# A ramp with x in transfers of 96 rows, its loads in another order, and roundings of the steps in two pieces

## The chip, the cores and the metric

The kernel runs on one core of one Trainium2 chip. The metric is the device time of one execution in microseconds, from the profiler; a kernel's time is the median of its runs.

## The reference, cut to what matters

A global filter in the frequency domain is followed by a two-layer perceptron with SiLU:

```python
X = np.fft.rfft(x, axis=1)                         # x: (8, 3008, 256), fp32
y = np.fft.irfft(X * (filt_r + 1j * filt_i)[None], n=3008, axis=1)
h = y.reshape(24064, 256) @ w_in                   # (256, 2048)
out = (h / (1 + exp(-h))) @ w_out                  # (2048, 256)
```

The weights `w_in` and `w_out` are float64 in memory; the kernel reads them as pairs of 32-bit words and rounds them to fp32 itself.

## The kernel before, in words

**Spectral part.** For each of the eight batches the transform of length 3008 = 2 x 47 x 32 is done in matrix products with tables. Stage 1 (`stage1`, line 308) multiplies x by a table `wx_t`; the results are copied out and written to a DRAM buffer d1 by the POOL queue (line 338). `load_t2` (line 404) reads them back in another order in six groups g; `forward` multiplies by the table `d_t` into banks `pb`, `multiply` (M) forms the products with the filters on VectorE (L433), `add` sums them (on GpSimd for batch 0, L441 and L442), `inverse` multiplies by `e_t` into banks `pc`, `even` copies (ScalarE, L465) and `rows` (VectorE, L473) forms sums and differences and sends them to a DRAM buffer d2. `load_t4` reads d2 and `stage3` (matrices `pd`) gives the tokens y.

**Perceptron.** The tokens of all batches are cut into 48 pairs of blocks; a pair takes eight steps, each with 128 x 2 columns of the hidden layer. Both products are done by Strassen's scheme with seven matrix products instead of eight: `hidden` (L611) and `project` (L670), whose instructions alternate in eight rounds per step. The pieces of the spectral part of the next batch are put into given steps and rounds by `put` and run by `until`.

**The ramp.** Batch 0 has nothing to hide behind: its spectral part, and the loading and rounding of the weights of the first nine column blocks j, are written out by hand ahead of the steps. The order of instructions on each engine is the order of the program text (a manual schedule). SyncE issues nearly all loads, so a load stands behind all loads written ahead of it; a transfer's issue also waits for the completion semaphore it takes over, of which there are eight, handed on in turn. `rounded(j)` calls `round_weights` (line 755): five operations on VectorE (L762, L764, L767, L768, L770), two on ScalarE (L763, L766), then two products that place the weights (L776, on GpSimd for j < 7, on VectorE from then on), and for odd j four combinations (`combine_weights`, L582). The blocks j = 9 to 15 are rounded inside steps 0 to 6, in round 1 of each.

**Batch 1.** Its x is loaded by `load_x` in eight pieces u, with the rows in two transfers of 64 and 32 rows; the first two are issued right ahead of step 0, the others by `stage1` itself, which stands in steps 0 to 7, round 3. `tokens` of pair 1 stands in step 6, round 1.

Of the kernel before, what the change touches and what calls it, by code (L numbers as in the profile page):

```python
# [55 lines left out]
NS, NG = 24, 6  # L56
# [35 lines left out]
def dft_tables():  # L92

    wf = np.zeros((128, 2, 64))
    for par in range(2):
        for i, idx in enumerate(ORDER):
            ph = 2 * np.pi * (np.arange(N1) * (2 * idx + par) % 94) / 94
            for h in range(2):
                wf[64 * h:64 * h + N1, par, 2 * i] = np.cos(ph)
                wf[64 * h:64 * h + N1, par, 2 * i + 1] = -np.sin(ph)  # L100

    wx = np.zeros((96, 2, 64))
    row = (np.arange(96) + 64) % 96
    for par in range(2):
        for i, idx in enumerate(ORDER):
            ph = 2 * np.pi * (row * (2 * idx + par) % 94) / 94
            wx[:, par, 2 * i] = np.where(row < 2 * N1, np.cos(ph), 0.0)
            wx[:, par, 2 * i + 1] = np.where(row < 2 * N1, -np.sin(ph), 0.0)  # L110

    wq = np.zeros((128, 4, 32))
    m = np.arange(24)
    for par in range(2):
        for i, idx in enumerate(ORDER):
            ph = 2 * np.pi * (m * (2 * idx + par) % 94) / 94
            for q in range(4):
                wq[32 * q:32 * q + 24, 2 * par, i] = np.where(m == 0, 0.5, np.cos(ph))  # L120
                wq[32 * q:32 * q + 24, 2 * par + 1, i] = -np.sin(ph)


    d = np.zeros((2, 2, 32, NS, 2, 32))
    n = np.arange(32)[:, None]
    for par in range(2):
        for i, idx in enumerate(ORDER):
            sp = 2 * idx + par
            kap = kept(sp)
            sg = np.where((kap - sp) % 94 == 0, 1.0, -1.0)  # L130
            k = np.where((kap - sp) % 94 == 0, kap, S - kap)
            th = 2 * np.pi * (n * k % S) / S
            d[par, 0, :, i, 0], d[par, 1, :, i, 0] = np.cos(th), np.sin(th)
            d[par, 0, :, i, 1], d[par, 1, :, i, 1] = -np.sin(th) * sg, np.cos(th) * sg


    e = np.zeros((4, 32, NG, 2, 2, 2, 32))
    n = np.arange(32)[None, :]
    for g in range(NG):
        for bank in range(2):  # L140
            for j in range(4):
                s = slot_residue(g, bank, j - j % 2)
                kap = kept(slot_residue(g, bank, j))
                sg = np.where((kap - s) % N1 == 0, 1.0, -1.0)[:, None]
                k = np.where((kap - s) % N1 == 0, kap, S - kap)[:, None]
                assert ((k - s) % 94 == (0 if j % 2 == 0 else N1)).all()
                th = 2 * np.pi * (n * k % S) / S
                e[j, :, g, bank, 0, 0], e[j, :, g, bank, 0, 1] = np.cos(th), np.sin(th)
                e[j, :, g, bank, 1, 0], e[j, :, g, bank, 1, 1] = -np.sin(th) * sg, np.cos(th) * sg


    wi = np.zeros((128, N1))
    for h in range(2):
        for i in range(NS):
            s = slot_residue(i // 4, i % 2, i // 2 % 2 * 2)
            ph = 2 * np.pi * ((2 * np.arange(N1) + h) * s % 94) / 94

            wi[64 * h + 2 * i] = 2 * np.cos(ph) / S if s else 1.0 / S
            wi[64 * h + 2 * i + 1] = -2 * np.sin(ph) / S if s else 0.0
    f32 = np.float32  # L160
    return (wf.astype(f32), wx.reshape(96, 128).astype(f32), wq.astype(f32), wi.astype(f32),
            d.reshape(128, NS, 2, 32).astype(f32),
            e.reshape(128, NG, 2, 2, 64).astype(f32))
# [3 lines left out]
def kernel(  # L167
# [51 lines left out]
    w_t = cpool.tile([128, 7, 2, NJP, 128], FP32)  # L219
    zero_t = w_t[:, S4, 0, NJP - 2:NJP].rearrange("p j n -> p (j n)")  # L220
    warm = cpool.tile([128, 1], FP32)
    bias_t = cpool.tile([128, 1], FP32)
    x_all = xpool.tile([128, 2, 2, 2 * C], FP32)
    x_t = [x_all[:, i] for i in range(2)]

# [37 lines left out]
    def spectral(b):  # L263
# [4 lines left out]

        def load_rows(view, u, n):


            for p0, r0, nr in ((32, 0, 64), (0, 64, 32)):
                nc.sync.dma_start(out=view[p0:p0 + nr],
                                  in_=bass.AP(tensor=x.tensor,
                                              offset=x.offset + (b * S + 32 * r0 + 4 * u) * C,
                                              ap=[[32 * C, nr], [1, 4 * n * C]]))

        def load_first():

            view = w_t.rearrange("p c w j n -> p (c w j n)")[:, 0:32 * C]  # L280
            for u, n in ((0, 2), (2, 2), (4, 4)):
                load_rows(view[:, 4 * C * u:4 * C * (u + n)], u, n)
            for u in range(8):
                xs[u] = view[:, 4 * C * u:4 * C * (u + 1)]
# [204 lines left out]
        def stage3(g):  # L489
# [3 lines left out]
            for cb in range(2):  # L493
                for i in range(4):
                    for c0 in (0, 64):
                        for h in range(2):
# [2 lines left out]
                                out=ps[h][c0:c0 + 64, cb, i, :],  # L499
                                lhsT=t4s[g][rows, i, 128 * cb + c0:128 * cb + c0 + 64],  # L500
                                rhs=wi_t[rows, :], start=True, stop=True)
            if g < 6 and (b > 0 or g > 1):
                load_t4(g + 2)
            if n0 == 0:
                y[b, half] = ypool.tile([128, 2, HALF], FP32, name=f"y_{b}_{half}", tag="y")
# [14 lines left out]
    def plan(b, part):  # L520
# [1 line left out]
        at = STEPS * b  # L522

        if b == 1:
            put(at - 51, 0, part["load_x"], 0)
            put(at - 51, 0, part["load_x"], 1)
            for u in range(8):
                put(at + u - 48, 3, part["stage1"], u)
        else:
# [225 lines left out]
    def round_weights(j):  # L755

        words = raws.pop(j).rearrange("p w (n t) -> p (w n) t", t=2)
        lo, hi = words[:, :, 0], words[:, :, 1]
        e = zpool.tile([128, 512], U32, name=f"e_{j}", tag="z")
        m = ppool.tile([128, 512], U32, name=f"m_{j}", tag="p")  # L760
        ef, mf = e.bitcast(FP32), m.bitcast(FP32)
        v.tensor_scalar(out=m, in0=hi, scalar1=0xfffff, scalar2=None, op0=ALU.bitwise_and)  # L762
        nc.scalar.activation(out=mf, in_=m, func=AFT.Identity, scale=2.0 ** -20, bias=1.0)  # L763
        v.tensor_scalar(out=e, in0=hi, scalar1=20, scalar2=0x7ff,  # L764
                        op0=ALU.logical_shift_right, op1=ALU.bitwise_and)
        nc.scalar.activation(out=ef, in_=e, func=AFT.Relu, bias=bias_t)  # L766
        v.scalar_tensor_tensor(out=mf, in0=lo, scalar=2.0 ** -52, in1=mf, op0=ALU.mult, op1=ALU.add)  # L767
        v.tensor_scalar(out=e, in0=ef, scalar1=255.0, scalar2=float(1 << 23),  # L768
                        op0=ALU.min, op1=ALU.mult)
        v.scalar_tensor_tensor(out=e, in0=hi, scalar=0x80000000, in1=e,  # L770
                               op0=ALU.bitwise_and, op1=ALU.bitwise_or)
        for w in range(2):
            cols = slice(256 * w, 256 * w + 256)
            dst = places(j, w) if w == 0 else places(j, w).rearrange("p k (q i) -> p k q i", q=4)
            eng = gp if j < 7 else v
            eng.tensor_tensor(out=dst, in0=columns(mf[:, cols], w), in1=columns(ef[:, cols], w),  # L776
                              op=ALU.mult)
        if j % 2:
            combine_weights(j // 2)
# [21 lines left out]
            if wide:  # L801
                load_weights(j)

    def rounded(j):
        if wide:
            round_weights(j)
        else:
            load_exact(j)

    def idle(n):  # L810
# [4 lines left out]

    def inverse_rows(part, g):
        part["inverse"](g)
        for i in range(2):
            part["even"](g, i)
            part["rows"](g, i)  # L820


    nc.sync.dma_start(out=wx_t, in_=wx_dram.ap())
    nc.vector.memset(zero_t, 0.0)
    nc.gpsimd.memset(bias_t, -896.0)
    nc.gpsimd.memset(x_all[96:128], 0.0)
    part = spectral(0)
    part["load_first"]()
    idle(6)
    nc.sync.dma_start(out=d_t[:, 0:8], in_=d_dram[:, 0:8])  # L830
    weights(0, 1)
    load_filters((nc.sync, nc.sync), 0, 4)
    weights(2, 3)
    for u in range(8):
        part["stage1"](u)
    for g in range(2):
        part["load_t2"](g)
    nc.sync.dma_start(out=d_t[:, 8:NS], in_=d_dram[:, 8:NS])
    nc.sync.dma_start(out=e_t, in_=e_dram.ap())
    for g in range(2, 4):  # L840
        part["load_t2"](g)
    for j in range(3):
        rounded(j)
    idle(16)
    for g in range(NG):
# [4 lines left out]
            part["add"](g, k)  # L850
        if g == 0:
            load_filters((nc.sync, nc.gpsimd), 4, 2 * NG)
            weights(4, 5)
        if g == 1:
            for t, dram in ((wi_t, wi_dram), (wf_t, wf_dram), (wq_t, wq_dram)):
                nc.sync.dma_start(out=t, in_=dram.ap())
        if g == 2:
            weights(6, 7, 8)
        if g > 0:
            inverse_rows(part, g - 1)  # L860
        idle(2)
# [3 lines left out]
    idle(12)  # L865
    for g in range(4):
        part["load_t4"](g)
    rounded(7)
    rounded(8)
    for g in range(4):  # L870
# [1 line left out]
    weights(9, 10, 11, 12, 13)  # L872
    early[0] = None
    plan_rest(0, part)
    for b in range(1, B):
        plan(b, spectral(b))
    for j in range(9, NJ):
        put(j - 9, 1, rounded, j)

        if j < 11:  # L880
            put(j - 9, 1, weights, j + 5)
# [5 lines left out]
    stores = (((10, 1), (10, 5)), ((19, 1), (23, 5)), ((31, 1), (31, 5)), ((35, 1), (35, 5)),  # L887
              ((43, 1), (43, 5)), ((50, 1), (51, 1)))
    for pair in range(len(pairs)):
        step, rnd = combines[pair % per]  # L890
        pending.append((pair // per * STEPS + step + rnd / ROUNDS, 98, lambda pair=pair: tokens(pair)))
        for chunk in range(2):
            step, rnd = stores[pair % per][chunk]
# [51 lines left out]
```

## Time and profile before

| | us |
|---|---|
| median of four runs | 2641.29 (2639.24 to 2644.06) |
| profiled execution | 2639.24 |
| its span | 2637.4 |
| PE busy | 2585.6 (98%) |
| DVE busy | 1700.7 (64%) |
| ACT busy | 1102.5 (42%) |
| POOL busy | 450.3 (17%) |
| mean granted clock | 0.986 |

The page divides the span into 40 slices of 66 us; the first two hold the ramp. A timeline row gives the start, the duration, the engine, the line, the operation with its tiles (`out<-in`), the number of instructions and, in brackets, the idle time of the engine before it with what released it. PE counts a matrix product of fp32 twice, as two passes. `SPq` and `ACTq` are the queues in which SyncE and ScalarE issue transfers.

### The profile page before, as it was taken

To read this page: it belongs to the slowest core of one execution; us is meant where nothing else is said; L and a number is where in the kernel's file an instruction comes from. 1 tells how busy PE (TensorE), PEld (TensorE's weight loads), DVE (VectorE), ACT (ScalarE), POOL (GpSimd) and SP (SyncE) were. 2 spreads that over 40 slices of the span, in tenths; PEclk is the share of its full clock that TensorE was granted. 3 is DMA by queue.
4 is the path that set the end of the run, shared out by engine and by line. 5 is a ranking of instruction groups with operands and counts; after the bars stand their busy time and mean duration, and the time that the engine had idled before them with its cause. 6 is when DMAs were issued, how large, how long until landed. Compare 5 with 4: busy or idle time off the path is not lost.

```text
span 2637.4 us, 48074 instructions
## 1 busy us (share of the span) xinstructions
PE 2585.6 (98%) x18748; PEld 2187.8 (83%) x18748; DVE 1700.7 (64%) x3585; ACT 1102.5 (42%) x3008; POOL 450.3 (17%) x692
## 2 busy tenths in 40 slices
PE   6799999999999999999999999999999999999998
PEld 3478888888888888888888888888888888888987
DVE  4666666667666666666666676666766666555554
ACT  1254344444444444444444444444444444444443
POOL 5211112211221111112111211121112111100100
PEclk8699999999999999999999999999999999999999
DMA  9632222322233123221222222232223311211000
GB/s 266 181 96 53 66 61 66 80 55 65 66 71 75 45 64 81 67 65 53 80 61 56 73 70 65 51 81 68 65 56 72 84 45 28 55 22 21 9 16 16
DMA packets 203659, 176.29 MB, mean 67 GB/s; under 512 B 122308, under 2 KB 176932, under 8 KB 202740
## 3 DMA queue, kind: packets, MB, share of 16 engines
q1 hardware_dynamic: 183144, 121.57, 19.3%
q0 software_dynamic: 17616, 48.52, 5.7%
q8 instruction: 147, 2.41, 0.4%
q10 hardware_dynamic: 2672, 3.13, 0.4%
q14 instruction: 80, 0.66, 0.1%
HBM read 98.15 MB, written 84.41 MB: 69 GB/s over the span
## 4 chain that ended last, share of the span: by engine, by line
PE 94%; DMA 3%; DVE 2%; SPq 1%; issue 0%; ACT 0%; POOL 0%; ACTq 0%; DVEq 0%
PE acc L670 43%; PE px L611 25%; PE pyz L611 19%; PE pd L498 3%; PE pb L421 2%; PE pc L454 2%; PE pf L388 1%; DMA raw<-in_moe_w_out_dram 1%; PE pa L330 0%; DMA x_all<-in_x_dram 0%; PE pa L321 0%; DMA d<-q 0%; DMA e_t<-e_tbl 0%; DMA w_t<-in_x_dram 0%; SPq L233 0%
## 5 line engine op out<-in xcount | busy, mean ns | idle before, releaser
L670 PE MATMUL acc<-g,w_t 128*128 128x256 f32 (+1 forms) x5376 | 1512.0, 375 | 0.4 <-DVE g L582 0.4
L670 PEld LDWEIGHTS acc<-g,w_t 128*128 128x128 f32 x5376 | 1021.3, 190 | 115.6 <-DVE g L582 0.8
L582 DVE TENSOR_TENSOR g<-pyz,abc 128x256 f32<-128x256 f32 (+1 forms) x1152 | 480.3, 417 | 551.7 <-ACT abc L632 304.5
L582 DVE TENSOR_TENSOR g<-g 128x256 f32<-128x256 f32 (+3 forms) x1152 | 617.0, 536 | 197.3 <-ACT g L615 184.1
L611 PE MATMUL px<-ty,w_t 128*128 128x256 f32 (+1 forms) x2304 | 686.9, 380 | 1.5 <-ACT abc L626 1.0
L615 ACT ACTIVATE g<-g 128x256 f32<-128x256 f32 (+1 forms) x1152 | 474.8, 412 | 246.1 <-DVE g L582 246.1
L582 POOL TENSOR_TENSOR s<-s 128x256 f32<-128x256 f32 (+1 forms) x329 | 259.8, 807 | 1453.5 <-DVE s L688 1373.0
L611 PEld LDWEIGHTS px<-ty,w_t 128*128 128x128 f32 x2304 | 424.1, 190 | 85.3 <-issue 25.9
L611 PE MATMUL pyz<-y,w_t 128*128 128x256 f32 (+1 forms) x1536 | 453.6, 377 | 2.9 <-DVE g L582 2.9
L611 PEld LDWEIGHTS pyz<-y,w_t 128*128 128x128 f32 x1536 | 283.7, 189 | 48.4 <-DVE g L582 7.9
L626 ACT COPY abc<-px 128x256 f32<-128x256 f32 (+1 forms) x384 | 141.8, 369 | 363.8 <-PE px L611 363.8
L615 ACT ACTIVATE g<-px 128x256 f32<-128x256 f32 (+1 forms) x384 | 146.5, 382 | 307.4 <-PE px L611 307.3
L632 ACT COPY abc<-px 128x256 f32<-128x256 f32 (+1 forms) x384 | 144.3, 376 | 309.2 <-PE px L611 309.2
L611 PE MATMUL px<-y,w_t 128*128 128x256 f32 (+1 forms) x768 | 229.8, 381 | 1.0 <-ACT y L246 1.0
L611 PE MATMUL pyz<-ty,w_t 128*128 128x256 f32 (+1 forms) x768 | 225.6, 375 | 0.0
L611 PEld LDWEIGHTS px<-y,w_t 128*128 128x128 f32 x768 | 142.1, 189 | 40.0 <-ACT g L615 15.5
L611 PEld LDWEIGHTS pyz<-ty,w_t 128*128 128x128 f32 x768 | 146.0, 190 | 16.9 <-DVE g L582 0.5
L619 ACT COPY abc<-px 128x256 f32<-128x256 f32 (+1 forms) x384 | 135.7, 353 | 2.7 <-PE px L611 1.3
L244 DVE COPY y<-pd 128x376 f32<-128x376 f32 x64 | 51.5, 805 | 103.1 <-PE pd L498 103.1
L246 ACT COPY y<-pd 128x376 f32<-128x376 f32 x64 | 51.8, 810 | 94.5 <-PE pd L498 94.5
L498 PEld LDWEIGHTS pd<-wi_t,t 48*64 48x64 f32 x4096 | 67.8, 137 | 24.2 <-issue 22.8
L498 PE MATMUL pd<-wi_t,t 48*64 48x47 f32 x4096 | 76.0, 236 | 3.9 <-DMA t<-d 2.2
(74 smaller groups left out, 1352.4 us busy)
## 6 DMA issues: line engine op xcount, KB each, us to landing
t<-d SPq DMA_DIRECT2D x96, 256.0 KB
t<-d SPq DMA_DIRECT2D x128, 192.0 KB
d<-q POOLq DMA_DIRECT2D x85, 256.0 KB, 2.6
out_dram<-o SPq DMA_DIRECT2D x636, 32.0 KB
d<-tf POOLq DMA_DIRECT2D x144, 96.0 KB, 2.4
d<-t POOLq DMA_DIRECT2D x52, 192.0 KB, 3.5
xr<-in_x_dram SPq DMA_DIRECT2D x6, 1472.0 KB
x_all<-in_x_dram SPq DMA_DIRECT2D x72, 96.0 KB
```

The source lines that it names most:

```text
L244: nc.vector.tensor_copy(out=dst, in_=src)
L246: nc.scalar.copy(out=dst, in_=src)
L421: nc.tensor.matmul(out=ps[k][32 * j:32 * j + 32, ri, :], lhsT=d_t[rows, 4 * g + at, ri, :], rhs=t2[rows, at, :], start=True, stop=True)
L454: nc.tensor.matmul(out=ps[j][64 * k:64 * k + 64, a, :], lhsT=e_t[rows, g + a, k, ri, :], rhs=zs[k][rows, ri, :], start=(a == 0 and ri == 0 ...
L498: nc.tensor.matmul(out=ps[h][c0:c0 + 64, cb, i, :], lhsT=t4s[g][rows, i, 128 * cb + c0:128 * cb + c0 + 64], rhs=wi_t[rows, :], start=True, ...
L582: eng.tensor_tensor(out=out, in0=in0, in1=in1, op=op)
L611: nc.tensor.matmul(out=out, lhsT=w_t[:, c, 0, jp], rhs=rhs, start=start, stop=True, skip_group_check=True)
L615: nc.scalar.activation(out=g[:, k, 0:n], in_=g[:, k, 0:n] if src is None else src, func=AFT.Silu)
L619: nc.scalar.copy(out=sums[:, 0, 0:n], in_=xo)
L626: nc.scalar.copy(out=sums[:, 1, 0:n], in_=xo)
L632: nc.scalar.copy(out=sums[:, 2, 0:n], in_=xo)
L670: nc.tensor.matmul(out=acc[pair][i][:, h, 0:n], lhsT=w_t[:, c, 1, jp], rhs=g[:, k, 0:n], start=(jp == 0 and h == 0), stop=last, skip_group ...
```

## The change

Five things change together:

- x of batches 0 and 1 is loaded in transfers of 96 rows instead of 64 and 32, and the table `wx` has its rows in natural order to fit. The first load of batch 0 is cut into pieces of 1, 1, 2 and 4 instead of 2, 2 and 4.
- The loads of the ramp stand in another order: the filters' first part ahead of all weights, three weight blocks ahead of t2 instead of four, then `e_t`, the filters' rest, the rest of `d_t`, t2 of groups 2 and 3, and weights 3 to 5; the three small tables one group later. The first two pieces of batch 1's x are issued after the t4 loads of groups 0 to 3 and ahead of weights 9 to 13; t4 of groups 4 and 5 go to step 7.
- In the ramp both `even` copies of a group stand ahead of its two `rows`.
- The clamp of the exponent for j < 9 is done by two activations on ScalarE instead of one operation (L768) on VectorE.
- `round_weights` ends ahead of the placing, which is now `place_weights`. In the steps the first part stays in round 1, the placing and combining go to round 5. `tokens` of pair 1 goes to step 7.

```diff
     wx = np.zeros((96, 2, 64))
-    row = (np.arange(96) + 64) % 96
+    row = np.arange(96)
     for par in range(2):
         for i, idx in enumerate(ORDER):
             ph = 2 * np.pi * (row * (2 * idx + par) % 94) / 94
...
     w_t = cpool.tile([128, 7, 2, NJP, 128], FP32)
     zero_t = w_t[:, S4, 0, NJP - 2:NJP].rearrange("p j n -> p (j n)")
     warm = cpool.tile([128, 1], FP32)
-    bias_t = cpool.tile([128, 1], FP32)
+    bias_t = cpool.tile([128, 3], FP32)
     x_all = xpool.tile([128, 2, 2, 2 * C], FP32)
     x_t = [x_all[:, i] for i in range(2)]
...
         def load_rows(view, u, n):
-            for p0, r0, nr in ((32, 0, 64), (0, 64, 32)):
-                nc.sync.dma_start(out=view[p0:p0 + nr],
-                                  in_=bass.AP(tensor=x.tensor,
-                                              offset=x.offset + (b * S + 32 * r0 + 4 * u) * C,
-                                              ap=[[32 * C, nr], [1, 4 * n * C]]))
+            nc.sync.dma_start(out=view[0:96],
+                              in_=bass.AP(tensor=x.tensor, offset=x.offset + (b * S + 4 * u) * C,
+                                          ap=[[32 * C, 96], [1, 4 * n * C]]))
         def load_first():
             view = w_t.rearrange("p c w j n -> p (c w j n)")[:, 0:32 * C]
-            for u, n in ((0, 2), (2, 2), (4, 4)):
+            for u, n in ((0, 1), (1, 1), (2, 2), (4, 4)):
                 load_rows(view[:, 4 * C * u:4 * C * (u + n)], u, n)
             for u in range(8):
                 xs[u] = view[:, 4 * C * u:4 * C * (u + 1)]
...
                                 out=ps[h][c0:c0 + 64, cb, i, :],
                                 lhsT=t4s[g][rows, i, 128 * cb + c0:128 * cb + c0 + 64],
                                 rhs=wi_t[rows, :], start=True, stop=True)
-            if g < 6 and (b > 0 or g > 1):
+            if g < 6 and (b > 0 or g > 3):
                 load_t4(g + 2)
             if n0 == 0:
                 y[b, half] = ypool.tile([128, 2, HALF], FP32, name=f"y_{b}_{half}", tag="y")
...
         at = STEPS * b
         if b == 1:
-            put(at - 51, 0, part["load_x"], 0)
-            put(at - 51, 0, part["load_x"], 1)
             for u in range(8):
                 put(at + u - 48, 3, part["stage1"], u)
         else:
...
         nc.scalar.activation(out=mf, in_=m, func=AFT.Identity, scale=2.0 ** -20, bias=1.0)
         v.tensor_scalar(out=e, in0=hi, scalar1=20, scalar2=0x7ff,
                         op0=ALU.logical_shift_right, op1=ALU.bitwise_and)
-        nc.scalar.activation(out=ef, in_=e, func=AFT.Relu, bias=bias_t)
+        nc.scalar.activation(out=ef, in_=e, func=AFT.Relu, bias=bias_t[:, 0:1])
         v.scalar_tensor_tensor(out=mf, in0=lo, scalar=2.0 ** -52, in1=mf, op0=ALU.mult, op1=ALU.add)
-        v.tensor_scalar(out=e, in0=ef, scalar1=255.0, scalar2=float(1 << 23),
-                        op0=ALU.min, op1=ALU.mult)
+        if j < 9:
+            nc.scalar.activation(out=ef, in_=ef, func=AFT.Relu, scale=-1.0, bias=bias_t[:, 1:2])
+            nc.scalar.activation(out=e, in_=ef, func=AFT.Identity, scale=-float(1 << 23), bias=bias_t[:, 2:3])
+        else:
+            v.tensor_scalar(out=e, in0=ef, scalar1=255.0, scalar2=float(1 << 23),
+                            op0=ALU.min, op1=ALU.mult)
         v.scalar_tensor_tensor(out=e, in0=hi, scalar=0x80000000, in1=e,
                                op0=ALU.bitwise_and, op1=ALU.bitwise_or)
+        raws[j] = mf, ef
+    def place_weights(j):
+        mf, ef = raws.pop(j)
+        eng = gp if j < 7 else v
         for w in range(2):
             cols = slice(256 * w, 256 * w + 256)
             dst = places(j, w) if w == 0 else places(j, w).rearrange("p k (q i) -> p k q i", q=4)
-            eng = gp if j < 7 else v
             eng.tensor_tensor(out=dst, in0=columns(mf[:, cols], w), in1=columns(ef[:, cols], w),
                               op=ALU.mult)
         if j % 2:
...
             if wide:
                 load_weights(j)
-    def rounded(j):
-        if wide:
+    def rounded(j, part=None):
+        if wide and part != 1:
             round_weights(j)
-        else:
+        if wide and part != 0:
+            place_weights(j)
+        if not wide and part != 1:
             load_exact(j)
     def idle(n):
...
     def inverse_rows(part, g):
         part["inverse"](g)
-        for i in range(2):
-            part["even"](g, i)
-            part["rows"](g, i)
+        for piece in ("even", "rows"):
+            for i in range(2):
+                part[piece](g, i)
     nc.sync.dma_start(out=wx_t, in_=wx_dram.ap())
     nc.vector.memset(zero_t, 0.0)
-    nc.gpsimd.memset(bias_t, -896.0)
+    for i, value in enumerate((-896.0, 255.0, 255.0 * (1 << 23))):
+        nc.gpsimd.memset(bias_t[:, i:i + 1], value)
     nc.gpsimd.memset(x_all[96:128], 0.0)
-    part = spectral(0)
+    part, second = spectral(0), spectral(1)
     part["load_first"]()
     idle(6)
     nc.sync.dma_start(out=d_t[:, 0:8], in_=d_dram[:, 0:8])
-    weights(0, 1)
     load_filters((nc.sync, nc.sync), 0, 4)
-    weights(2, 3)
+    weights(0, 1, 2)
     for u in range(8):
         part["stage1"](u)
     for g in range(2):
         part["load_t2"](g)
-    nc.sync.dma_start(out=d_t[:, 8:NS], in_=d_dram[:, 8:NS])
     nc.sync.dma_start(out=e_t, in_=e_dram.ap())
-    for g in range(2, 4):
-        part["load_t2"](g)
     for j in range(3):
         rounded(j)
     idle(16)
...
             part["add"](g, k)
         if g == 0:
             load_filters((nc.sync, nc.gpsimd), 4, 2 * NG)
-            weights(4, 5)
-        if g == 1:
+            nc.sync.dma_start(out=d_t[:, 8:NS], in_=d_dram[:, 8:NS])
+            for later in (2, 3):
+                part["load_t2"](later)
+            weights(3, 4, 5)
+        if g == 2:
+            weights(6, 7, 8)
             for t, dram in ((wi_t, wi_dram), (wf_t, wf_dram), (wq_t, wq_dram)):
                 nc.sync.dma_start(out=t, in_=dram.ap())
-        if g == 2:
-            weights(6, 7, 8)
         if g > 0:
             inverse_rows(part, g - 1)
         idle(2)
...
     idle(12)
     for g in range(4):
         part["load_t4"](g)
+    for u in range(2):
+        second["load_x"](u)
     rounded(7)
     rounded(8)
     for g in range(4):
...
     weights(9, 10, 11, 12, 13)
     early[0] = None
     plan_rest(0, part)
+    for g in (4, 5):
+        put(7, 0, part["load_t4"], g)
     for b in range(1, B):
-        plan(b, spectral(b))
+        plan(b, second if b == 1 else spectral(b))
     for j in range(9, NJ):
-        put(j - 9, 1, rounded, j)
+        put(j - 9, 1, rounded, j, 0)
+        put(j - 9, 5, rounded, j, 1)
         if j < 11:
             put(j - 9, 1, weights, j + 5)
...
     stores = (((10, 1), (10, 5)), ((19, 1), (23, 5)), ((31, 1), (31, 5)), ((35, 1), (35, 5)),
               ((43, 1), (43, 5)), ((50, 1), (51, 1)))
     for pair in range(len(pairs)):
-        step, rnd = combines[pair % per]
+        step, rnd = combines[pair % per] if pair != 1 else (7, 1)
         pending.append((pair // per * STEPS + step + rnd / ROUNDS, 98, lambda pair=pair: tokens(pair)))
         for chunk in range(2):
             step, rnd = stores[pair % per][chunk]
```

## Prediction

> **What bounds the kernel now.** I read the page first, then the busy times of four stretches.
>
> ```profile
> PE   6799999999999999999999999999999999999998
> DMA  9632222322233123221222222232223311211000
> ```
> ```profile
> 0.00:112.00 112.00, 80.55 (x764) 47.27 (x765) 62.62 (x118) 25.00 (x44) 49.82 (x79) 0.77 0.81 228
> 112.00:192.00 80.00, 70.45 (x267) 51.05 (x268) 53.00 (x122) 37.31 (x92) 8.25 (x16) 0.92 0.40 122
> 192.00:2600.00 2408.00, 2407.98 (x17590) 2065.40 (x17589) 1567.79 (x3305) 1028.61 (x2840) 391.98 (x596) 1.00 0.23 58
> ```
>
> The second column is PE's busy time, the last three are clock, DMA share and GB/s. From 192 us on PE idles 0.02 us of 2408, and the change touches nothing there. All that can move lies in the first 192 us, where DMA is the busiest unit (81%) and PE waits. So I read that part in order of time, first PE's timeline:
>
> ```profile
> 112.03 1.19 PE L611 MATMUL px<-y,w_t 128*128 128x256 f32 x2 [0.98 <-ACT y L246]
> ...
> 120.98 3.75 PE L321 MATMUL pa<-x_all,wx_t 96*128 96x512 f32 x4 [5.10 <-DMA x_all<-in_x_dram]
> ...
> 143.23 0.70 PE L611 MATMUL pyz<-y,w_t 128*128 128x256 f32 x2 [0.97 <-DVE g L582]
> ...
> 174.78 0.70 PE L611 MATMUL px<-ty,w_t 128*128 128x256 f32 x2 [1.04 <-ACT abc L626]
> ```
>
> The steps begin at 112.03; 3.9 us later PE stands 5.10 us for x of batch 1; later steps lose about a microsecond at 143.23, 160.07, 174.78 and 178.44. Before 112 VectorE and the transfers set the pace. DVE's timeline:
>
> ```profile
> 60.27 0.69 DVE L433 TENSOR_TENSOR z<-pb,filt 128x512 f32<-128x512 f32 x1 [4.75 <-DMA filt<-in_filt_i_dram]
> ...
> 65.14 0.42 DVE L762 TENSOR_SCALAR m<-raw 128x512 uint32<-128x512 uint32 x1
> 65.47 0.42 DVE L764 TENSOR_SCALAR e<-raw 128x512 uint32<-128x512 uint32 x1
> 66.29 0.69 DVE L767 SCALAR_TENSOR_TENSOR m<-raw,m 128x512 f32<-128x512 uint32 x1 [0.40 <-ACT m L763]
> 66.91 0.43 DVE L768 TENSOR_SCALAR e<-e 128x512 uint32<-128x512 f32 x1
> 67.37 0.69 DVE L770 SCALAR_TENSOR_TENSOR e<-raw,e 128x512 uint32<-128x512 uint32 x1
> ...
> 81.64 0.93 DVE L762 TENSOR_SCALAR m<-raw_y 128x512 uint32<-128x512 uint32 x1 [1.03 <-POOL z L442]
> ```
>
> I call the products of group g M(g), its sums with the copies R(g), the rounding of column j r(j). M(2) begins at 60.27, held by a filter transfer; M(3), M(4), M(5) follow at 67.97, 75.67 and 85.36. Nothing catches up after that: R(5) gives the last d2 transfer, then come the t4 loads, then stage 3.
>
> **Roundings ahead of the steps.** The clamp L768 (0.46 us from its start to the next) leaves DVE, nine times. But DVE runs in order and L770 now waits for two more activations in series behind L766. From r(4)'s start at 65.14: ACT took L763 at +0.48, L766 at +1.02 for 0.71. Two more of 0.71, each with some 0.05 to start, end at +3.25; L770 starts at +3.3 and frees DVE at +3.9. Before it was 67.97 - 65.14 = 2.83. So a rounding costs 1.1 us more, not 0.46 less; the bounds are -0.46 (where DVE came late anyway) and +1.5 (activations not overlapped at all). Queued behind L770 on DVE is the next M(g).
>
> **Both copies first.** DVE's two pairs of R(g) had a gap of about 0.81 us, because the second copy stood behind the first d2 transfer on ACT. That goes: -0.8 per group. R(5) had its copies together already, so nothing there.
>
> **Loads by order of need, to M(2).** The 16 filter transfers (0.6 us of issue each) now precede the raw weights. The built program has eight completion semaphores for these transfers, and each issue waits for the transfer eight places before it: in SP's timeline the filter issue that needed x's last piece went out at 16.66. I leave that time for x's last chunk; in the new order it holds the seventh filter, ten issues later SP is at 22.5, and raw 0 lands about 27 (estimate: by the trace's landing marks the filters issued at 24.1 to 26.8 took 2.9 to 4.3 us). r(0) to r(2): 27 + 3 x 3.9 = 38.7; with POOL beside them up to 40.4 (r(6) with POOL beside its first operations took 3.72, against 2.83). t2 comes earlier: it was issued at 32.64 and pb began 6.1 later; now the last d1 write (issued at 25.30, 3.6 to land) allows it at 29, pb(0) is done by 35, and the roundings are what is late next. M(0): 39, before 41.97. Then POOL places r(2) (1.4), adds (4 x 0.69): 43.3; pc 1.3, copy 0.4, R(0) 1.7: the d2 transfers issue at 45.6 and 46.4 (before 49.13 and 50.83).
>
> Now a new wait. In the built program the two loads t2(2) take the semaphores of these two d2 transfers, and t2(3) and raw 3 stand behind them on SP. How long such a transfer takes is bounded by the SP queue's timeline: its filter issue at 56.95 waited for the one issued at 49.13, 7.8 us; a lone one, by ACT's wait at 82.61, about 2.
>
> ```profile
> 51.01 0.58 SPq L233 DMA_DIRECT2D filt<-in_filt_i_dram  x1
> 56.95 0.55 SPq L233 DMA_DIRECT2D filt<-in_filt_r_dram  x1
> ```
>
> I take 3, nearer the lone one since SP's queue is empty by then: 49.4. Behind it four t2 halves at 1.15 and raw 3's two at 0.7 land by 56.3; r(3) 3.9; M(2) at 60.2. Before: 60.27. The filter wait of 4.75 goes and the wait for raw 3 takes its place: **0 us** (bounds -4, if M(0) is at 35 and the landing 2; +5.7, if it is 7.8).
>
> On this the Trainium skill, "DMA: Bandwidth & Descriptors", section "Issuing engines are not separate DMA queues", says that transfers of all issuers share the same 16 engines and another issuer saves only its issue time. The 7.8 against 2 agrees. By it alone the reordering gives nothing while the engines are full, and this term is 0 too; where they stand empty behind a semaphore, it is silent.
>
> **M(2) to M(5).** Before 25.1. After: M 2.4, R 1.7, and r(4) may not write m before POOL has read the products of M(2); POOL first places r(3) and combines (1.4 + 2.9), which before was over by 60.0 and now begins at M(2), then two adds: r(4) starts at +5.75, ends at +10.6 with POOL's 0.9; M(3) and R(2) to +14.7; r(5) to +18.8; M(4), R(3) to +23; r(6) waits for POOL the same way, from +24.6 to +29.4. That is +4.3; without POOL's 0.9 twice +2.5. I take **+3.5** (bounds -1 and +6). From M(5) to 112.03 nothing is shortened. r(7) and r(8) take 2 us more, covered: DVE was through them at 102.8 and the last stage-3 copy waited until 111.1. Uncovered they would cost those 2. First x 0.39 MB at a time: PE's 2.04 us wait before its first pa may shrink by 0 to 2, hidden behind the raws.
>
> **x of batch 1.** Issued right behind the eight t4 loads, ahead of ten weight transfers: 0.8 MB more lands some 5 us before it is used. The 5.10 go. The clock adds to it: it was 0.50 from 112 to 124 and 0.92 from 124 to 128, and the four pa took 3.75 against 1.88 later. Without the gap PE warms up earlier, so up to 1.9 more. r(9), hidden in the gap before, now meets step 0 (about 1 against). **-6.2**, bounds -7.0 and -4.
>
> The skill's "TensorE: Matmul & The Clock Gate", section "What's actually happening", has a free-running window of about 3.4 us that must be busy before full speed returns. By it PE is slow for 3.4 to 6.8 us from the steps' start, against some 7.5 before, so this term would be 5.1 + 0.3 to 2.0; the rows with 0.50 and 0.92 agree with two speeds, and can't show where a window begins.
>
> **Steps.** With the products at round 5, g2 comes before them, so the 0.97 of three odd steps loses its cause. But DVE in such a step still has 2.9 (r) + 0.4 + 2.3 + g's and differences = 8.2 us, and a step with its pa is 7.8; the next rounding starts late, ACT's copy L626 stands behind it, and PE waits there instead (as at 174.78). The combine moved from step 6 to 7 takes 1.5 us off the worst step. Of 3.9 idle I count **-2.0** (bounds 0 and -5, the idle and its restarts).
>
> **Sum:** 0 + 3.5 - 6.2 - 2.0 = -4.7. The profiled execution took 2639.24 (span 2637.4), the median of four is 2641.29; on the median: **2636.6**.
>
> **Rivals.** *Front gains (0.28):* the roundings lie beside transfers, M(0) comes at 35, M(2) at 56.5, the later chain loses 1: -2.8 - 6.2 - 3.5 = -12.5, 2629. For it: 10 us of DMA order is improved ahead of M(0); against: L770's place on DVE. *Slower (0.10):* one mechanism, t2(2) behind the d2 transfers: if these take 7.8 as at 49.13, M(2) is at 65 to 66 and all later terms stay, +5.7 + 4.3 - 6.2 - 0 = +3.8, 2645; it turns slower than before where the front loses over 8.2. *It doesn't do it (0.10):* x still lands late behind the t4 loads, 3 us of wait left: about 2640.5.
>
> **How the numbers follow.** The forecast has 0.52, by itself 2630 to 2642. A measurement tells 0.2% (5.3 us), so faster means under 2636.0: 0.27 of the first rival and 0.20 of the forecast, 0.47; slower, over 2646.6: 0.07, from the second rival; same 0.46. The range takes in the first rival's middle and the second's: 2627.5 to 2645.
>
> **What would show it.** M(2) waiting for raw 3 or r(3) instead of a filter; SP standing for d2 ahead of t2(2); L770 waiting about 1.5 us for ACT; the first px near 115.5; no x wait; px waiting on L626 after odd steps. First px under 110 makes the front's working wrong; an x wait over 2 us, or stalls as before at pyz, the other terms.

## The result, and the profile after

The changed kernel took 2646.72 us (median of 36 runs, 2644.98 to 2649.36) against 2640.85 us for the kernel before on the same chips: ratio 1.0021, 95% interval 1.0016 to 1.0025. So it is 5.9 us slower, where 4.7 us less had been forecast. The profiled execution took 2647.04 us, with a span of 2645.3 us.

First, what the whole page and the stretches say. The fence holds two rows of the page's 40 slices.

```profile
PE   6699999999999999999999999999999999999998
DMA  8632222222223123221232222222223311211000
```

The next rows are busy times by stretch of the changed kernel; after the length come PE, PEld, DVE, ACT and POOL, at the end clock, DMA share and GB/s.

```profile
112.00:192.00 80.00, 69.47 (x491) 51.41 (x491) 56.72 (x130) 38.07 (x88) 7.22 (x14) 0.89 0.55 150
192.00:2600.00 2408.00, 2408.00 (x17588) 2065.01 (x17587) 1567.19 (x3303) 1030.00 (x2843) 392.97 (x598) 1.00 0.23 59
...
52.00:57.00 5.00, 0.00 (x0) 0.00 (x0) 0.00 (x0) 0.00 (x0) 3.44 (x6) 0.78 0.97 256
57.00:66.00 9.00, 5.11 (x67) 2.32 (x68) 0.00 (x0) 0.00 (x0) 0.00 (x0) 0.55 0.83 227
```

From 192 us on PE does not idle, as before. The loss lies in the ramp, and the last two rows show its place: from 52 to 66 us VectorE and ScalarE do nothing at all, and for the first five of these PE does nothing either, while the DMA engines are 97% and 83% busy. The transfers are on the move, but not the ones that are needed next. VectorE's timeline gives the wait its name:

```profile
66.42 0.43 DVE L757 TENSOR_SCALAR m<-raw 128x512 uint32<-128x512 uint32 x1 [14.48 <-DMA raw<-in_moe_w_out_dram]
...
69.67 0.69 DVE L770 SCALAR_TENSOR_TENSOR e<-raw,e 128x512 uint32<-128x512 uint32 x1 [1.43 <-ACT e L766]
70.28 0.68 DVE L430 TENSOR_TENSOR z<-pb,filt 128x512 f32<-128x512 f32 x1
```

r(3) stands 14.48 us for raw 3, and M(2), queued behind it, comes at 70.28 instead of 60.27. SyncE's queue says why raw 3 was so late:

```profile
48.22 0.57 SPq L857 DMA_DIRECT2D d_t<-d_tbl  x1
56.83 3.43 SPq L407 DMA_DIRECT2D t<-d  x4
60.31 0.60 SPq L744 DMA_DIRECT2D raw<-in_moe_w_in_dram  x1
60.96 0.47 SPq L747 DMA_DIRECT2D raw<-in_moe_w_out_dram  x1
```

Between 48.8 and 56.83 us SyncE issues nothing. It holds t2(2), which takes over the semaphore of the first d2 transfer; raw 3 is four issues behind. The summary of SyncE's waits up to 62 us (line, what it waited for, us in total, times, longest) agrees:

```profile
SPq L233 <- DMA w_t<-in_x_dram: 9.6, 3, 6.0
SPq L407 <- DMA d<-q: 8.9, 2, 8.0
SPq L407 <- DMA d<-t: 4.4, 3, 2.4
```

The chain of waits of the changed kernel, read from 51.97 us, runs along this path up to the issue of raw 3:

```profile
51.97 6.35 DMA d<-q
58.33 0.61 SPq L407
...
60.31 0.60 SPq L744
```

From there the chain goes on with the transfers of raw 4 and later weights. The last link is read from VectorE's row above and from the trace's landing mark (the time at which a transfer's completion is signalled): the second half of raw 3, issued at 60.96, landed at 66.30, and r(3) began at 66.42.

The last view is PE's timeline at the start of the steps:

```profile
128.57 1.19 PE L606 MATMUL px<-y,w_t 128*128 128x256 f32 x2 [0.98 <-ACT y L246]
...
132.22 2.44 PE L318 MATMUL pa<-x_all,wx_t 96*128 96x512 f32 x4
...
138.66 0.70 PE L606 MATMUL pyz<-y,w_t 128*128 128x256 f32 x2 [0.75 <-DVE g L577]
155.24 0.70 PE L606 MATMUL pyz<-y,w_t 128*128 128x256 f32 x2 [0.62 <-DVE g L577]
```

The steps begin 16.5 us later than before. The wait of 5.10 us for x of batch 1 is gone and the pa take 2.44 us instead of 3.75; the later stalls are a little shorter than before (0.62 where 0.97 stood). From the first px to the end of the span it is 2516.7 us instead of 2525.4. So the steps give 8.7 us back, close to the 8.2 forecast for them, and the ramp itself loses much more than forecast.

### The profile page after: what moved, and what is told of

Read it like the earlier page. It is cut to its first block, busy times and chain, and to the rows that moved or that the text cites. A ratio compares the mean times of both kernels' runs of the same rounds, so it can differ in the third digit from the quotient of the medians.

```text
span 2645.3 us, 48073 instructions
## 1 busy us (share of the span) xinstructions
PE 2590.1 (98%) x18748; PEld 2189.0 (83%) x18748; DVE 1697.8 (64%) x3576; ACT 1114.2 (42%) x3026; POOL 451.1 (17%) x694
## 4 chain that ended last, share of the span: by engine, by line
PE 94%; DMA 2%; DVE 2%; ACT 1%; issue 1%; SPq 1%; POOL 0%; DVEq 0%; ACTq 0%; POOLq 0%
PE acc L665 43%; PE px L606 25%; PE pyz L606 18%; PE pd L495 3%; PE pc L451 2%; PE pb L418 2%; PE pf L385 1%; DMA d_t<-d_tbl 1%; PE pa L327 0%; DMA d<-q 0%; DMA raw<-in_moe_w_out_dram 0%; PE pa L318 0%; DVE g L577 0%; DMA raw_y<-in_moe_w_out_dram 0%; DVE w_t L577 0%
## 5 line engine op out<-in xcount | busy, mean ns | idle before, releaser
L606 PEld LDWEIGHTS px<-ty,w_t 128*128 128x128 f32 x2304 | 423.9, 190 | 82.9 <-issue 25.1
```

The lines of the kernel that those rows point to most:

```text
L606: nc.tensor.matmul(out=out, lhsT=w_t[:, c, 0, jp], rhs=rhs, start=start, stop=True, skip_group_check=True)
```

## The experiments

Each kernel was timed beside the kernel before. The medians are of 11 runs, but of ten for "before + x early", of five for "old loads and clamp" and "before + all three", of 56 for before and 36 for after. The table has the milestones of each profiled execution, in us from the start of its span, with the letters of the prediction. A profile is one execution: M(2) of the run with only the steps changed came 1.6 us earlier than before though nothing ahead of it differs, so single milestones are read to about 2 us, the medians more closely.

| kernel | median | ratio (95%) | M(0) | M(2) | M(5) | first px |
|---|---|---|---|---|---|---|
| before | 2640.85 | | 41.97 | 60.27 | 85.36 | 112.03 |
| after | 2646.72 | 1.0021 (1.0016 to 1.0025) | 43.08 | 70.28 | 99.79 | 128.57 |
| old loads | 2633.93 | 0.9974 (0.9965 to 0.9983) | 43.00 | 62.40 | 89.34 | 117.40 |
| old clamp | 2642.71 | 1.0006 (0.9997 to 1.0014) | 42.89 | 68.71 | 95.75 | 124.51 |
| old loads and clamp | 2631.68 | 0.9965 (0.9952 to 0.9977) | 42.85 | 61.39 | 84.95 | 114.20 |
| t2 ahead | 2643.43 | 1.0010 (1.0001 to 1.0019) | 44.39 | 66.85 | 96.78 | 125.89 |
| raw 3 early | 2640.68 | 0.9998 (0.9989 to 1.0006) | 45.67 | 67.58 | 94.97 | 123.35 |
| t2 ahead, raw 3 early | 2636.56 | 0.9982 (0.9973 to 0.9991) | 44.30 | 61.94 | 89.79 | 118.00 |
| raw 0 early | 2646.69 | 1.0022 (1.0013 to 1.0031) | 42.44 | 68.83 | 98.52 | 127.37 |
| x in 2, 2, 4 | 2646.66 | 1.0023 (1.0014 to 1.0032) | 43.68 | 68.35 | 97.83 | 127.03 |
| before + x early | 2635.11 | 0.9977 (0.9968 to 0.9986) | 42.62 | 61.71 | 86.76 | 115.75 |
| before + two pieces | 2639.34 | 0.9989 (0.9980 to 0.9998) | 40.98 | 58.65 | 83.81 | 112.65 |
| before + copies | 2637.57 | 0.9988 (0.9979 to 0.9996) | 40.05 | 57.66 | 81.22 | 108.72 |
| before + all three | 2629.52 | 0.9956 (0.9943 to 0.9968) | 41.70 | 60.87 | 84.45 | 111.48 |

### Which part costs: the loads or the clamp

The theory was that the new order of loads puts raw 3 behind the d2 transfers; the rival, that the clamp's two extra activations hold VectorE. Each was undone alone, and then both. First the loads:

```diff
-    load_filters((nc.sync, nc.sync), 0, 4)
-    weights(0, 1, 2)
+    weights(0, 1)
+    load_filters((nc.sync, nc.sync), 0, 4)
+    weights(2, 3)
...
+    nc.sync.dma_start(out=d_t[:, 8:NS], in_=d_dram[:, 8:NS])
     nc.sync.dma_start(out=e_t, in_=e_dram.ap())
+    for g in range(2, 4):
+        part["load_t2"](g)
...
             load_filters((nc.sync, nc.gpsimd), 4, 2 * NG)
-            nc.sync.dma_start(out=d_t[:, 8:NS], in_=d_dram[:, 8:NS])
-            for later in (2, 3):
-                part["load_t2"](later)
-            weights(3, 4, 5)
-        if g == 2:
-            weights(6, 7, 8)
+            weights(4, 5)
+        if g == 1:
             for t, dram in ((wi_t, wi_dram), (wf_t, wf_dram), (wq_t, wq_dram)):
                 nc.sync.dma_start(out=t, in_=dram.ap())
+        if g == 2:
+            weights(6, 7, 8)
```

> The changed kernel with the loads of the ramp in the order of before (weights 0 and 1 ahead of the filters, weights 2 and 3 ahead of t2, d_t and t2 of groups 2 and 3 ahead of the filters' second part); everything else stays changed. Loads theory (the front was lost because raw 0 comes late behind the filters and because t2(2), t2(3) and raw 3 stand behind the first two d2 transfers): M(2) from 70.3 back to about 61, the steps' start from 128.6 to about 119, the median some 9 us under the changed kernel, about 2637.5. Clamp theory (the front was lost because L770 waits for two more activations): M(2) stays at 68 or later, the median within 2 us of the changed kernel, about 2645.

It took 2633.93 us, 12.8 less than the changed kernel, and 3.6 less than the loads theory had expected. In VectorE's timeline of this run M(2) waits for a filter again, as in the kernel before:

```profile
62.40 0.69 DVE L430 TENSOR_TENSOR z<-pb,filt 128x512 f32<-128x512 f32 x1 [4.83 <-DMA filt<-in_filt_i_dram]
```

Then the clamp alone:

```diff
-        if j < 9:
-            nc.scalar.activation(out=ef, in_=ef, func=AFT.Relu, scale=-1.0, bias=bias_t[:, 1:2])
-            nc.scalar.activation(out=e, in_=ef, func=AFT.Identity, scale=-float(1 << 23), bias=bias_t[:, 2:3])
-        else:
-            v.tensor_scalar(out=e, in0=ef, scalar1=255.0, scalar2=float(1 << 23),
-                            op0=ALU.min, op1=ALU.mult)
+        v.tensor_scalar(out=e, in0=ef, scalar1=255.0, scalar2=float(1 << 23),
+                        op0=ALU.min, op1=ALU.mult)
```

> The changed kernel with the clamp on VectorE as before (L768 back, the two activations gone); the loads stay in the new order. Loads theory: each rounding is 1.1 us shorter, three of them ahead of M(0), one ahead of M(2), three between M(2) and M(5): M(2) at 66, the steps' start 4 to 8 us earlier, the median 2639 to 2643. Clamp theory: most of the 16.5 us by which the steps start later goes, the median 2634 or less.

2642.71 us, 4.0 less than the changed kernel, within the range of the loads theory; M(2), at 68.71, came later than its 66. The wait for raw 3 is still there in VectorE's timeline, and nearly as long:

```profile
65.90 0.43 DVE L757 TENSOR_SCALAR m<-raw 128x512 uint32<-128x512 uint32 x1 [14.13 <-DMA raw<-in_moe_w_out_dram]
```

And both undone (the two diffs together):

> The changed kernel with the ramp's old order of loads and the old clamp on VectorE: what is left of the change is x in transfers of 96 rows with the first load in 1, 1, 2 and 4, both copies first, x of batch 1 early and the roundings of the steps in two pieces. The same with x in two transfers took 2629.5. With the old order of loads but the new clamp it was 2633.9. If the clamp costs under the old order about what the prediction's working gives (4.3 from M(2) to M(5), less the filter wait ahead of it), this run is at 2629 to 2631; if the clamp only cost time because raw 3 came late, it is at 2633 to 2635. x in 96 rows by itself: within 1 us of the run with two transfers.

2631.68 us, just above the 2629 to 2631 expected if the clamp has a cost of its own. The four corners give a table of their own:

| us | old clamp | new clamp | clamp costs |
|---|---|---|---|
| old loads | 2631.68 | 2633.93 | 2.3 |
| new loads | 2642.71 | 2646.72 | 4.0 |
| loads cost | 11.0 | 12.8 | |

The order of loads costs 11 to 13 us, the clamp 2 to 4; the 2.3 is the less certain, since the intervals of its two runs overlap. From M(2) to M(5) the times are 23.6 (both old), 26.9 (clamp new), 27.0 (loads new) and 29.5 (both new): the clamp costs 2.5 to 3.4 there. The rival is a real cost, but a fifth to a third of the other.

### What in the order of loads costs it

If raw 3 and t2(2) are late because they stand behind the d2 transfers, taking one or the other ahead of them should give back a part, and both nearly all. First t2:

```diff
+    nc.sync.dma_start(out=d_t[:, 8:NS], in_=d_dram[:, 8:NS])
     nc.sync.dma_start(out=e_t, in_=e_dram.ap())
+    for g in range(2, 4):
+        part["load_t2"](g)
...
             load_filters((nc.sync, nc.gpsimd), 4, 2 * NG)
-            nc.sync.dma_start(out=d_t[:, 8:NS], in_=d_dram[:, 8:NS])
-            for later in (2, 3):
-                part["load_t2"](later)
             weights(3, 4, 5)
```

> The changed kernel, with the rest of d_t and t2 of groups 2 and 3 put back ahead of e_t and the filters' second part (as in the kernel before); weights 3 to 5 and all else stay where the change put them. Theory 'a load behind the d2 transfers' (t2(2), t2(3) and raw 3 stand on SP until the d2 transfers of group 0 land, at 56.8 and 58.3): now only a filter and raw 3 stand behind them, raw 3 lands some 4 us earlier (four t2 issues of about 0.65 to 1.15 us and their transfer time), M(2) comes at 65 to 66 and not at 70.3, and the time is 4 to 5 us under the changed kernel, 2641 to 2643. Rival 'late start' (the 10 us come from x's last transfer and raw 0 ahead of M(0)): t2 is not what is late, M(2) stays above 69 and the time within 1.5 us of the changed kernel, 2645 to 2648.

2643.43 us, 3.3 less than the changed kernel, and M(2) 3.4 earlier: less than the 4 to 5 expected, since two filter issues now stand where the t2 issues stood (56.80 and 57.40, raw 3 behind them at 58.98). Then raw 3 alone:

```diff
-    weights(0, 1, 2)
+    weights(0, 1, 2, 3)
...
-            weights(3, 4, 5)
+            weights(4, 5)
```

> The changed kernel with one block of weights moved: raw 3 is loaded with raws 0 to 2 ahead of t2, not behind t2(2) and t2(3). The d2 transfers still hold t2(2) on SP. Theory 'raw 3 at the end of the queue that waits for d2': r(3) is done before 55, M(2) waits only for pb(2), which began at 60.24 in the changed kernel, so M(2) comes at 60.5 to 62, 8 to 10 us earlier, and the time is 2637 to 2640. Rival 'everything behind d2 is late alike' (t2(2) or the filters bind as well): M(2) not before 66, time 2643 or more.

2640.68 us, 6.0 less, a little above the range that the theory gave, and M(2) at 67.58 instead of 60.5 to 62. What is late next is t2(2); the rows are from PE's and from VectorE's timeline of this run:

```profile
64.45 3.07 PE L418 MATMUL pb<-t,d_t 64*32 64x256 f32 x32 [9.80 <-DMA t<-d]
```
```profile
67.58 0.69 DVE L430 TENSOR_TENSOR z<-pb,filt 128x512 f32<-128x512 f32 x1 [6.03 <-PE pb L418]
```

So the rival held for half of it: two loads that M(2) needs stand behind d2, and moving one leaves the other. M(2) gains 2.7 us, and 2.1 more come by M(5): r(4) starts at 71.74, right behind R(1), where it stood 1.91 us in the changed kernel. Both together:

```diff
-    weights(0, 1, 2)
+    weights(0, 1, 2, 3)
...
+    nc.sync.dma_start(out=d_t[:, 8:NS], in_=d_dram[:, 8:NS])
     nc.sync.dma_start(out=e_t, in_=e_dram.ap())
+    for g in range(2, 4):
+        part["load_t2"](g)
...
             load_filters((nc.sync, nc.gpsimd), 4, 2 * NG)
-            nc.sync.dma_start(out=d_t[:, 8:NS], in_=d_dram[:, 8:NS])
-            for later in (2, 3):
-                part["load_t2"](later)
-            weights(3, 4, 5)
+            weights(4, 5)
```

> The changed kernel with all that M(2) needs, but the filters, ahead of the d2 transfers on SP: raw 3 with raws 0 to 2, and the rest of d_t and t2 of groups 2 and 3 ahead of e_t. Of the new order of loads only the filters' first part ahead of raws 0 to 3 is left. By themselves t2 ahead gave 3.3 and raw 3 ahead 6.0 us. Theory 'what stands on SP behind the d2 transfers': with both, M(2) waits for a filter again, as in the kernel before and in the run with the old loads: M(2) 61 to 64, first px 117 to 120, time 2634 to 2637 (the old order of loads gave 2633.9). Rival 'filters ahead of raw 0' (raw 0 at 30 to 33 and M(0) at 45 carry the loss on): M(2) 66 or later and 2639 or more.

2636.56 us, 10.2 less than the changed kernel, and inside the expected 2634 to 2637. VectorE's timeline has the filter wait back, and only a short one:

```profile
61.94 0.69 DVE L430 TENSOR_TENSOR z<-pb,filt 128x512 f32<-128x512 f32 x1 [1.74 <-DMA filt<-in_filt_i_dram]
```

Of the 12.8 us that the order of loads costs, 10.2 thus come back when raw 3 and t2 of groups 2 and 3 (with the rest of `d_t`) stand ahead of the d2 transfers. The remaining 2.6, between two runs whose intervals overlap, belong to what is left of the order: the filters ahead of raws 0 and 1, and the later place of the small tables. These two were not separated. That taking raw 0 alone ahead gains nothing is shown by the next run:

```diff
-    load_filters((nc.sync, nc.sync), 0, 4)
-    weights(0, 1, 2)
+    weights(0)
+    load_filters((nc.sync, nc.sync), 0, 4)
+    weights(1, 2)
```

> The changed kernel with raw 0 alone loaded ahead of the filters' first part, as in the kernel before. The changed kernel's raw 0 landed at 30.45, and r(0) to r(2) stood one after another on VectorE ahead of M(0) at 43.08. Theory 'a late raw 0 moves the whole chain': raw 0 lands at 20 to 24, r(0) starts 6 us earlier, but raws 1 and 2 come as late as before, so M(0) comes 3 to 4 us earlier (39 to 40), the d2 transfers go out as much earlier, and with them t2(2), raw 3 and M(2): 66 to 67, time 2642 to 2644. Rival: M(0) is held by pb(0) or by raw 2 instead, or the d2 transfers land at 57 to 58 whenever they go out, since the 16 filter transfers and the rest of d_t are in the way: M(2) at 69 to 70, time within 1.5 of 2646.7.

2646.69 us: nothing gained, the rival's outcome. r(0) starts at 25.62 instead of 30.54, but r(1) then stands 4.40 us for raw 1, as VectorE's timeline says, and M(0) comes 0.6 us earlier:

```profile
34.29 0.43 DVE L757 TENSOR_SCALAR m<-raw 128x512 uint32<-128x512 uint32 x1 [4.40 <-DMA raw<-in_moe_w_out_dram]
...
64.98 0.43 DVE L757 TENSOR_SCALAR m<-raw 128x512 uint32<-128x512 uint32 x1 [14.27 <-DMA raw<-in_moe_w_out_dram]
```

Its two d2 transfers went out 1.2 us earlier and landed 2 to 3.3 us earlier, and still raw 3 was waited for as long. The pieces of x's first load do nothing either:

```diff
-            for u, n in ((0, 1), (1, 1), (2, 2), (4, 4)):
+            for u, n in ((0, 2), (2, 2), (4, 4)):
```

> The changed kernel, with the first load of x in pieces of 2, 2 and 4 as before, still in 96 rows. Pieces of 1 and 1 let PE begin 1.6 us earlier (6.50 against 8.07), but PE then waits 2.96 us for the last piece in either case, so I expect no change that can be measured: first px within 0.7 us of 128.6, 2645.5 to 2648. If the pieces of 1 and 1 were what made the last piece of x land late (17.07), it would land at 16.6 or earlier and M(0) come 0.5 us earlier: 2646.

2646.66 us, as expected. First px came 1.5 us earlier in its profile, where 0.7 at most had been expected, with no trace of that in the medians, which shows how far a single profile may be trusted.

### The parts that were to gain

Each was put into the kernel before by itself. x of batch 1 early:

```diff
-            if g < 6 and (b > 0 or g > 1):
+            if g < 6 and (b > 0 or g > 3):
...
-            put(at - 51, 0, part["load_x"], 0)
-            put(at - 51, 0, part["load_x"], 1)
...
-    part = spectral(0)
+    part, second = spectral(0), spectral(1)
...
     for g in range(4):
         part["load_t4"](g)
+    for u in range(2):
+        second["load_x"](u)
...
+    for g in (4, 5):
+        put(7, 0, part["load_t4"], g)
```

> The kernel before, with one part alone: the first two pieces of batch 1's x are issued right behind the t4 loads of groups 0 to 3, t4 of groups 4 and 5 in step 7. The step of the prediction: the 5.10 us wait goes and the array is warm earlier, -6.2, about 2634.6, first px still near 112. Rival: the t4 loads and the raw weights set when step 0 can go on, so a new wait takes its place: less than 2 us gained, 2639 or more.

2635.11 us, 5.9 less than the kernel before beside it. In its profile the first px came at 115.75 and not near 112; the gain lies behind it. PE's timeline of this run has no wait ahead of the first pa:

```profile
115.75 1.19 PE L609 MATMUL px<-y,w_t 128*128 128x256 f32 x2 [0.99 <-ACT y L246]
...
119.40 2.12 PE L321 MATMUL pa<-x_all,wx_t 96*128 96x512 f32 x4
```

The roundings of the steps in two pieces, with `place_weights` split off as in the change:

```diff
-        put(j - 9, 1, rounded, j)
+        put(j - 9, 1, rounded, j, 0)
+        put(j - 9, 5, rounded, j, 1)
...
-        step, rnd = combines[pair % per]
+        step, rnd = combines[pair % per] if pair != 1 else (7, 1)
```

> The kernel before, with one part alone: roundings of the steps in two pieces, the tokens of pair 1 in step 7. The step of the prediction: 2 us of the stalls go (from the four near 1 us, some come back as waits for L626), about 2639. Rival: the stalls go altogether, 4 to 5 us, 2636; or VectorE is full in the odd steps and nothing is gained, 2641.

2639.34 us, 1.6 less (ratio 0.9980 to 0.9998). Both copies first:

```diff
-        for i in range(2):
-            part["even"](g, i)
-            part["rows"](g, i)
+        for piece in ("even", "rows"):
+            for i in range(2):
+                part[piece](g, i)
```

> The kernel before, with both even copies of a group ahead of its two sums in the ramp; nothing else. By the prediction a gap of 0.8 us per group goes from DVE in R(0) to R(4): of these two or three lie ahead of M(2), which a filter transfer holds at 60.27, so they give nothing, and two or three lie between M(2) and M(5): first px 1.6 to 2.4 us earlier (109.6 to 110.4), time 1.5 to 2.5 us under the kernel before. If POOL's sums and the roundings' tiles hold that chain instead, it gives under 0.5 us.

2637.57 us, 3.0 less, a little above the 1.5 to 2.5 expected; 23.6 us from M(2) to M(5) instead of 25.1. And the three together, which is the version to keep:

> The kernel before, with three parts of the change: x of batch 1 early, the roundings of the steps in two pieces (with the tokens of pair 1 in step 7), both copies first. Old loads of the ramp, old clamp, x in two transfers. The first two gave -5.9 and -1.6 us by themselves and touch different steps, so together -7.5, with the copies -7.5 to -9.5: 2631 to 2634, ratio 0.9965 to 0.997. If the two share a cause (the steps catch up either way), -6: 2635.

2629.52 us, ratio 0.9956 (0.9943 to 0.9968): 11.1 us less than the kernel before, where the three by themselves add up to 10.5; 2631 to 2634 had been expected. It has the lowest median of this study. The version with both loads and clamp as of old differs from it only in x of 96 rows with its first pieces, and took 2631.68 us; the two intervals overlap, so whether 96 rows cost 2 us or nothing stays open. From the kernel before to the changed one the medians thus go -11.3 (these three, against the 2640.85 of all runs), +2.2 (x, open), +11.0 (loads), +4.0 (clamp): +5.9.

## Why the prediction was wrong

**The step that failed is "Loads by order of need, to M(2): 0 us"**; it was +10.0 in this profile, and +8.1 and +8.6 in those of two runs with the same median (x in 2, 2, 4 and raw 0 early). Its path was right link by link (raw 0, three roundings, the d2 transfers, t2(2), raw 3, r(3), M(2)), and its sizes were not:

- M(0) at 39: measured 43.08 (+4.1). The raw weights reached SyncE at 25.06 instead of 22.5. The last piece of x let SyncE go on at 17.08, near the 16.66 that had been left for it, but then the first part of `d_t` held it for another 1.0 us, and the ten issues took about 0.7 us each instead of 0.6. Raw 0 landed 5.4 us after its first issue instead of 4.5, at 30.45 instead of 27, and the three roundings took 12.5 us instead of 11.7. Raw 1 was late as well: with raw 0 early r(1) still starts at 34.29, against 34.53 here.
- M(0) to the second d2 issue: 8.9 us instead of 7.4 (+1.5). The chain of waits has it on GpSimd, which combines r(0) and r(1) until 44.4 before it places r(2) and adds; the prediction counted no combining here.
- The landing of that transfer: 6.35 us instead of 3 (+3.4). This was the choice between the rows of 7.8 and about 2, and it went to the wrong one: "SP's queue is empty by then" left out the eight filter transfers that POOL issues from 48.49 to 52.7, and the rest of `d_t`, issued at 48.22 and landed only at 53.74. The last of the filters landed at 58.08, beside the d2 transfers at 56.82 and 58.32. In three other runs in which the same loads go out right ahead of it (old clamp, x in 2, 2, 4, raw 0 early) this transfer took 4.65, 4.66 and 5.63 us, so some of the 3.4 belongs to this one execution.
- From there to raw 3's landing 8.0 instead of 6.9 (+1.1), and r(3) as said (3.9). The terms named for the 6.9, four times 1.15 and twice 0.7, add up to 6.0 only.

4.1 + 1.5 + 3.4 + 1.1 is the whole of the 10 us between 60.2 and 70.28. The bound of +5.7 was drawn too tight: it took the worst of one term, the landing, with the others as estimated, and all four came out late. (With 7.8 in place of 3 the working gives M(2) at 65.0, which is +4.7 and not +5.7.)

**M(2) to M(5), +3.5.** The working came to 29.4 us and 29.51 was measured; the discount to +3.5 was not earned. The parts behave as said: r(3) took 3.9, L770 waited 1.43 us for ScalarE, r(4) and r(6) each started after a wait of 1.9, right at the end of GpSimd's second sum (76.21 and 94.99), though the profile names a transfer as what released them. The clamp is no relief for VectorE, but a cost of 2.3 to 4.0 us in all.

**M(5) to the first px, "nothing is shortened".** It took 28.78 us, before 26.67. But the kernel with only the steps changed took 28.84, and the other runs 27.0 to 29.3. Nothing ahead of the first px differs between before and the kernel with only the steps changed, so the profile of before lies at the short end of what executions scatter. A sum built on one execution carried some 2 us of that.

**x of batch 1, -6.2:** right, -5.9 by itself. PE's clock did as the four pa show: 2.44 us at 132.22, between the 3.75 and 1.88 of before, so full speed came about 1.1 us into them (estimate: 1.1 + (1 - 1.1/3.75) x 1.88 = 2.44), 4.8 us after the steps' start. The granted clock agrees: 0.50 from 126 to 132, 0.67 from 132 to 134, 1.00 from 134 to 136. The 4.8 us lie within the 3.4 to 6.8 us that the prediction estimated from the window in the Trainium skill's "TensorE: Matmul & The Clock Gate", section "What's actually happening". **Steps, -2.0:** right in size, -1.6, but not in its picture: the wait is not taken over by px behind L626, whose 1.04 us at 174.78 have gone too; what remains is pyz behind the products on VectorE, 0.62 us where 0.97 stood.

**The rivals.** The slower one, t2(2) behind the d2 transfers, named the mechanism, its place and its price (M(2) at 65 to 66, 2645 us), and was given 0.10. The result lies 1.7 us beyond it, since M(0) was late as well. "Front gains" fell: the transfers ahead of M(0) were put in another order, not shortened. The Trainium skill's page "DMA: Bandwidth & Descriptors", section "Issuing engines are not separate DMA queues", says that transfers of all issuers interleave on the same 16 engines; the 6.35 us beside POOL's filters, against 2.02 and 2.54 from issue to landing for the d2 transfers issued at 93.14 and 107.71 in the changed kernel, agree.

## What to carry to other kernels

Where completion semaphores are handed on in turn, each load can stand behind a write that depends on the computation; look for the write's place in that turn, and keep every load that the next stage needs ahead of it. When an operation is moved to another engine to relieve one, count the latency it adds where the relieved engine runs in order and waits for the result. When several uncertain links of a chain follow each other, add their bounds up, and do not take one at its worst with the rest as estimated.

## What the runs showed of the hardware that was not expected

- The first two d2 transfers, the same in every run, took from 3.6 us (issued at 49.95 with raw 0 early) to 8.5 us (issued at 49.88 with the three parts together). That the filter transfers under way make the difference is argued from the landing marks, not tried by itself. All of them landed between 53.5 and 60.2 us, though they went out from 46.6 to 54.6.
- Dependent activations on a 128x512 tile follow each other in 0.75 us on ScalarE (108.62, 109.36, 110.11), so the clamp's two made VectorE wait 1.2 to 1.8 us at L770, for 0.46 us saved there.
- The DMA engines being busy is no sign that the right thing is moving: 97% from 52 to 57 us, with no compute engine but GpSimd at work.
